# Moving parts of a weight conversion from ScalarE and VectorE to GpSimd and ScalarE, and chunk 1's attention behind chunk 0's, in a windowed attention with a feed-forward layer

## The chip, the cores and the metric

The kernel runs on one core of a Trainium2 chip. The metric is the device time of one execution in microseconds (us). The core's engines run side by side, each in its own order: PE multiplies matrices, DVE (VectorE), ACT (ScalarE) and POOL (GpSimd) work on tiles, and SP (SyncE) has nothing to do but to begin transfers. An engine starts an instruction only when the one before it in its order has started and everything that it needs is there.

## The reference

`q`, `k`, `v` have 8 batches, 8 heads, 576 positions and 64 features; `w_in` is 512 x 2048 and `w_out` 2048 x 512.

```python
scores = (q @ k.T) / sqrt(D) + slope[h] * -(i - j)      # kept where 0 <= i - j < 128
attn = softmax(scores) @ v
x = attn.transpose(0, 2, 1, 3).reshape(4608, 512)
h = x @ w_in
g = where(h >= 1, h, where(h <= -1, 0, (h + 1) ** 2 / 4))
out = g @ w_out
```

All tensors come in as 64-bit floats and the result is float32. The kernel reads a 64-bit number as two 32-bit words, a low one and a high one. `q`, `k` and `v` are used in float32 as they are loaded; only the weights are unfolded from the two words.

## The kernel before, in words

The 4608 tokens are worked in 12 chunks of 384 (`CH`). A chunk has 4 pairs of heads. For a pair: scores by PE (`scores`, L443; chunks from 2 on L459), the exponential with its maximum and sum by DVE and ACT (`soften`, L482 to L495), the transpose of the attention weights by PE (`weights_t`, L504), their copy by ACT (L508) and two masks by POOL (L509, L511), and the product with `v` by PE (`values`, L538). The four results of a chunk are its `x`, which is split into a high and a low half-precision part (L583, L584).

The feed-forward layer goes through 16 blocks of 128 hidden features. `layer1` makes 12 products (L590 to L592), the activation is done by ACT (L597) and DVE (L598, L599), and `layer2` adds 3 products (L619 in chunk 0, L622 to L624 later) into three accumulators.

The weights are converted while chunk 0 runs, block by block, and stay in memory. For a block `fc`: `fetch_weights` loads 512 KB of `w_in` and 512 KB of `w_out` into one of three buffers (`raw`, L173, L175, begun by ACT); `unfold` turns the high words (L180) and the low words (L181) on ACT; `float32_of` joins them on DVE (L185, once for `w_in` and once for `w_out`); DVE takes each row's largest magnitude of `w_in` (L194). `scale_in` finds the block's power of two: PE spreads the 128 row values over all partitions (`across`, L152), DVE takes the maximum and makes a scale of it (L159 to L163, L202). `split_in` then makes the two half-precision parts that `layer1` multiplies with (ACT L210, DVE L211). ACT adds up the magnitudes of `w_out`'s rows (L219).

The order on each engine is set by a list scheduler from the order in which the program is emitted and from "issue after" marks (`behind`). `segments` is the list of attention steps, `ready[c]` says how many of them chunk c's feed-forward layer needs, and the loop at the end spreads the next chunk's segments over the current chunk's 32 half steps. `EARLY` names the attention heads of chunk 0 behind which the first three blocks are converted; a later block `fc` is converted behind the activation of block `fc - 3` (`convert_after`). At the start PE runs idle transposes (`keep_busy`, L88).

## Time and profile before

| | us |
|---|---|
| median of 3 runs | 993.35 (991.59 to 994.22) |
| the profiled execution's own time | 991.8 |
| its span, first to last instruction | 989.7 |
| PE busy | 955.0 (96%) |
| DVE busy | 731.6 (74%) |
| ACT busy | 607.2 (61%) |
| POOL busy | 340.6 (34%) |

A busy PE says only that a matmul was under way. Three stages are told apart below: A, up to 44 us, is chunk 0's attention; B, from 44 to 152 us, is chunk 0's feed-forward layer with the conversion of the weights and chunk 1's attention; C is the rest, eleven chunks in which all weights are ready.

### The profile page before, as it was taken

The page shows a single profiled execution, that of the slowest core. Times are in us where ns is not written, and L with a number is a line of the kernel's source. Part 1 is how long each engine was busy: PE and PEld are TensorE (multiplying, and loading weights), DVE is VectorE, ACT ScalarE, POOL GpSimd, SP SyncE. Part 2 cuts the span into 40 slices and gives each one's busy share as a digit, 9 for nine tenths or more (in the row PEclk, how much of TensorE's full clock was granted, in tenths as well). Part 3 has the DMA queues.
Part 4 walks back from the last instruction along what each step waited for, and adds up shares of the span by engine and source line. Part 5 has one row for each costly group of instructions (what it writes and reads, how often), then busy time and mean ns, then how long its engine had stood idle before and what let it go on. Part 6 is the DMA issues. An engine that isn't in the chain of part 4 may idle for free.

```text
span 989.7 us, 17764 instructions
## 1 busy us (share of the span) xinstructions
PE 955.0 (96%) x6181; PEld 522.2 (53%) x6181; DVE 731.6 (74%) x2089; ACT 607.2 (61%) x1509; POOL 340.6 (34%) x446
## 2 busy tenths in 40 slices
PE   8798899998999999999999999999999999999997
PEld 5444344554555555555555555555555555555553
DVE  6899798896787787687787788677677886765332
ACT  6788777666656666565665665666666655644322
POOL 5311003333334432532533533433443443334221
PEclk9799999998999999999999999999999999999999
DMA  8476441012021011112111101111201000000000
GB/s 274 134 245 201 154 141 39 12 49 72 30 59 58 25 41 63 38 30 60 62 33 52 58 25 54 63 30 50 72 30 30 33 1 1 33 2 1 33 1 32
DMA packets 53290, 59.86 MB, mean 60 GB/s; under 512 B 3408, under 2 KB 42576, under 8 KB 53200
## 3 DMA queue, kind: packets, MB, share of 16 engines
q1 hardware_dynamic: 42304, 41.82, 13.7%
q10 hardware_dynamic: 10896, 16.91, 4.9%
q8 instruction: 48, 0.79, 0.3%
q14 instruction: 42, 0.34, 0.1%
HBM read 49.28 MB, written 9.44 MB: 59 GB/s over the span
## 4 chain that ended last, share of the span: by engine, by line
PE 85%; DVE 7%; ACT 4%; DMA 1%; issue 1%; POOL 1%; ACTq 0%; SPq 0%; POOLq 0%; DVEq 0%
PE h L590 12%; PE h L592 12%; PE h L591 12%; PE acc L622 12%; PE acc L623 12%; PE acc L624 12%; PE s L459 5%; PE x L561 4%; PE p L504 3%; ACT z L484 1%; PE acc L619 1%; DMA vn<-in_v_dram 1%; DVE g L598 1%; ACT raw L181 1%; DVE g L599 1%
## 5 line engine op out<-in xcount | busy, mean ns | idle before, releaser
L607 POOL TENSOR_TENSOR gl<-g,gh 128x384 f16<-128x384 f32 x176 | 167.2, 950 | 453.5 <-ACT gh L606 442.7
L598 DVE SCALAR_TENSOR_TENSOR g<-u,half 128x384 f32<-128x384 f32 x176 | 123.9, 705 | 157.1 <-ACT u L597 144.1
L606 ACT CAST gh<-g 128x384 f16<-128x384 f32 x176 | 89.6, 509 | 189.2 <-DVE g L599 102.1
L622 PE MATMUL acc<-wo,gh 128*128 128x512 f16 x528 | 200.3, 379 | 0.0
L623 PE MATMUL acc<-wo,gh 128*128 128x512 f16 x528 | 200.2, 379 | 0.0
L624 PE MATMUL acc<-wo,gl 128*128 128x512 f16 x528 | 196.0, 379 | 0.0
L597 ACT ACTIVATE u<-h,shift,fall 128x384 f32<-128x384 f32 x176 | 116.4, 663 | 98.9 <-PE h L592 98.9
L484 ACT ACTIVATE z<-z,nmax 128x256 f32<-128x256 f32 (+2 forms) x288 | 137.7, 480 | 33.1 <-DVE nmax L482 31.1
L590 PE MATMUL h<-x,wi 128*128 128x384 f16 x384 | 125.8, 329 | 4.6 <-ACT x L570 2.8
L590 PE MATMUL h<-xh,wi 128*128 128x384 f16 x384 | 125.2, 327 | 4.3 <-ACT wi L210 2.9
L592 PE MATMUL h<-xh,wi 128*128 128x384 f16 x384 | 125.3, 326 | 1.1 <-DVE wi L211 1.1
L592 PE MATMUL h<-x,wi 128*128 128x384 f16 x384 | 126.1, 328 | 0.0
L591 PE MATMUL h<-x,wi 128*128 128x384 f16 x384 | 126.0, 328 | 0.0
L591 PE MATMUL h<-xl,wi 128*128 128x384 f16 x384 | 125.4, 327 | 0.0
L482 DVE CUSTOM_DVE_ANT_0 z<-s,near,z_of 128x256 f32<-128x256 f32 (+2 forms) x240 | 98.6, 459 | 33.7 <-PE s L459 33.5
L599 DVE SCALAR_TENSOR_TENSOR g<-h,gain,g 128x384 f32<-128x384 f32 x176 | 108.1, 615 | 3.9
L590 PEld LDWEIGHTS <-wi 128*128 128x128 f16 x768 | 75.2, 98 | 67.1 <-issue 7.5
L591 PEld LDWEIGHTS <-wi 128*128 128x128 f16 x768 | 75.4, 98 | 59.1 <-issue 7.2
L592 PEld LDWEIGHTS <-wi 128*128 128x128 f16 x768 | 75.3, 98 | 53.9 <-issue 3.6
L519 POOL TENSOR_SCALAR_AFFINE_SELECT lu<-lu 128x768 f16<-128x768 f16 x80 | 70.4, 894 | 58.2 <-DVE lu L517 57.7
L624 PEld LDWEIGHTS <-gl 128*128 128x128 f16 x528 | 51.5, 98 | 59.0 <-issue 0.4
L622 PEld LDWEIGHTS <-gh 128*128 128x128 f16 x528 | 51.6, 98 | 51.0 <-issue 1.1
(148 smaller groups left out, 1445.7 us busy)
## 6 DMA issues: line engine op xcount, KB each, us to landing
out_dram<-o SPq DMA_DIRECT2D x35, 256.0 KB, 2.1
raw<-in_moe_w_in_dram ACTq DMA_DIRECT2D x16, 512.0 KB, 4.6
raw<-in_moe_w_out_dram ACTq DMA_DIRECT2D x16, 512.0 KB, 5.5
vn<-in_v_dram SPq DMA_DIRECT2D x32, 256.0 KB, 2.8
qk<-in_q_dram SPq DMA_DIRECT2D x40, 192.0 KB, 2.4
qk<-in_k_dram SPq DMA_DIRECT2D x28, 256.0 KB, 2.8
vn<-in_v_dram SPq DMA_DIRECT2D x16, 192.0 KB, 2.6
qk<-in_k_dram SPq DMA_DIRECT2D x12, 192.0 KB, 2.5
```

What stands on the lines that cost most here:

```text
L482: a = V.tensor_tensor_reduce(out=z[:, i, c0:], in0=pt[:, n, c0:], in1=r[:, c0:], op0=ALU.add, op1=ALU.min, scale=factor, scalar=3.0e38, ac ...
L484: b = S.activation(z[:, i, c0:], z[:, i, c0:], AF.Exp, bias=nmax[:, i:i + 1], scale=-1.0, accum_out=sm[:, i, 0:1])
L590: T.matmul(ph, wi[fc][:, 0, cc, :], xh, start=(cc == 0), stop=False)
L591: T.matmul(ph, wi[fc][:, 0, cc, :], xl, start=False, stop=False)
L592: T.matmul(ph, wi[fc][:, 1, cc, :], xh, start=False, stop=(cc == NCC - 1))
L597: first = S.activation(u, ph, AF.Relu, bias=shift[c] if c else quarter, scale=fall[c][:, col])
L598: V.scalar_tensor_tensor(g, u, half[c] if c else 0.5, u, ALU.min, ALU.mult)
L599: last = V.scalar_tensor_tensor(g, ph, gain[c][:, col] if c else fall[c][:, col], g, ALU.mult, ALU.max)
L607: G.tensor_tensor(gl, g, gh, ALU.subtract)
L622: T.matmul(a, gh[:, ts], wo[fc][:, 0], start=first, stop=False)
L623: T.matmul(a, gh[:, ts], wo[fc][:, 1], start=False, stop=False)
L624: T.matmul(a, gl[:, ts], wo[fc][:, 0], start=False, stop=last)
```

## The change

Five things change.

1. The low words of a block are scaled by POOL (`G.tensor_scalar`, 128 x 1024, unsigned integers in, integers out) and no longer by ACT.
2. All loads of weights are begun by SP, in one queue with the loads of `q`, `k` and `v`; block 0's are issued behind the loads of the first two pairs, with no wait for one of them to land. For blocks 1 and 2 a memset of two words by POOL holds the load to its place.
3. The rows of `w_in` are bounded by the sum of magnitudes, added up by ACT as for `w_out`, and no longer by their maximum on DVE. This gives another power of two, and so other roundings.
4. From block 2 on the power of two is found for two blocks at once, behind every second activation.
5. `values` of pairs 2 and 3 and the steps that chunk 0 still needs are emitted ahead of chunk 1's first scores; the maxima of chunk 1's `v` for pairs 4 to 7 are emitted together, after pair 4. `EARLY` is (2, 3, 4, 5, 6, 7) in place of (2, 3, 4, 5, 7, 8).

```diff
@@ -170,40 +170,52 @@
 
     def fetch_weights(fc):
         w = raw[fc] = rawp.tile([P, 2, DM, 2], I32, name=f"raw{fc}", tag=f"raw{fc % 3}")
-        S.dma_start(w[:, 0].rearrange("p (c f) w -> p c f w", c=NCC),
-                    wi32[:, 2 * fc * P:2 * (fc + 1) * P].rearrange("(c p) (f w) -> p c f w", p=P, w=2))
-        S.dma_start(w[:, 1], wo32[fc * P:(fc + 1) * P, :].rearrange("p (f w) -> p f w", w=2))
+        if 0 < fc < 3:
+            G.memset(w[:1, :, 0, :1], 0)
+        DMA.dma_start(w[:, 0].rearrange("p (c f) w -> p c f w", c=NCC),
+                      wi32[:, 2 * fc * P:2 * (fc + 1) * P].rearrange("(c p) (f w) -> p c f w", p=P, w=2))
+        DMA.dma_start(w[:, 1], wo32[fc * P:(fc + 1) * P, :].rearrange("p (f w) -> p f w", w=2))
 
     def unfold(fc, which=slice(0, 2)):
 
         low, high = raw[fc][:, which, :, 0], raw[fc][:, which, :, 1]
         S.activation(high.bitcast(F32), high.bitcast(F32), AF.Prelu, scale=2.0 ** -112, alpha=2.0 ** 32)
-        S.activation(low, low.bitcast(U32), AF.Copy, scale=0.9375 * 2.0 ** -29)
+        G.tensor_scalar(low, low.bitcast(U32), 0.9375 * 2.0 ** -29, None, ALU.mult)
 
     def float32_of(fc, a, out):
 
         V.scalar_tensor_tensor(out.bitcast(I32), raw[fc][:, a, :, 1], 3, raw[fc][:, a, :, 0], ALU.logical_shift_left, ALU.bitwise_or)
 
-    wide = {}
+    wide, rows_i = {}, {}
 
     def convert_in(fc):
         f = wide[fc] = wp.tile([P, DM], F32, name=f"f_i{fc}", tag="f_i", bufs=3)
         unfold(fc)
         float32_of(fc, 0, f)
-        rows = column(f"rows_i{fc}", "rows")
-        V.tensor_reduce(rows, f, X, ALU.max, apply_absolute_value=True)
-        spread(f"i{fc}", rows)
+        if fc < 2 or fc % 2 == 0:
+            width = 1 if fc < 2 else 2
+            rows_i[fc] = column(f"rows_i{fc}_{width}", f"rows{width}", n=width)
+        S.activation(junk, f, AF.Abs, accum_out=rows_i[fc] if fc < 2 else rows_i[fc - fc % 2][:, fc % 2:fc % 2 + 1])
 
     def scale_in(fc):
-        s1, i1 = s_in[:, fc:fc + 1], i_in[:, fc:fc + 1]
-        scale_of(f"i{fc}", s1, i1)
-
-    def fall_in(fc):
-        V.tensor_scalar(fall[0][:, fc:fc + 1], i_in[:, fc:fc + 1], i_x[0], 0.25, ALU.mult, ALU.mult)
+        rows = rows_i.pop(fc)
+        n = rows.shape[1]
+        s1, i1 = s_in[:, fc:fc + n], i_in[:, fc:fc + n]
+        b = bank(f"m_i{fc}")[:, :n * P]
+        across(b, rows)
+        top = column(f"top_i{fc}", f"top{n}", n=n)
+        V.tensor_reduce(top, b.rearrange("p (a w) -> p a w", w=P), X, ALU.max)
+        ti = top.bitcast(I32)
+        V.tensor_scalar(ti, ti, 0x7F800000, None, ALU.bitwise_and)
+        V.tensor_scalar(i1, top, 2.0 ** -100, 1.0 / TOP, ALU.max, ALU.mult)
+        V.reciprocal(s1, i1)
+        if fc > 1:
+            fall_in(fc, n)
+
+    def fall_in(fc, n=1):
+        V.tensor_scalar(fall[0][:, fc:fc + n], i_in[:, fc:fc + n], i_x[0], 0.25, ALU.mult, ALU.mult)
 
     def split_in(fc):
-        if fc > 1:
-            fall_in(fc)
         f, s1 = wide.pop(fc), s_in[:, fc:fc + 1]
         t = wp.tile([P, 2, DM], F16, name=f"wi{fc}", tag=f"wi{fc}")
         wi[fc] = t.rearrange("p s (c f) -> p s c f", c=NCC)
@@ -653,6 +665,12 @@
         turned[m] = len(segments)
 
     for p in range(p8):
+        if p == NPAIR:
+            segments.append([lambda p=p: values(p - 2)])
+            turn(2 * p - 2)
+            turn(2 * p - 1)
+            segments.append([lambda p=p: values(p - 1)])
+            ready.append(len(segments))
         segments += [[lambda p=p: scores(p, (0, 1))], [lambda p=p: scores(p, (2,))]]
         if p < NPAIR:
             segments.append([lambda p=p: behind([scored_at[p]], lambda: keep_busy(KEEP[2 if p else 1]))])
@@ -660,22 +678,21 @@
             segments.append([lambda p=p: in_turn(p + 1)] + ([lambda p=p: load_qk(p + 2)] if p + 2 < p8 else []))
         if p == NPAIR + 1:
             segments.append([lambda: scale_x(1)])
-        if 2 <= p <= NPAIR:
+        if 2 <= p < NPAIR:
             segments.append([lambda p=p: values(p - 2)])
-        if 1 <= p <= NPAIR:
+        if 1 <= p < NPAIR:
             turn(2 * p - 2)
             turn(2 * p - 1)
         if p >= NPAIR:
-            segments.append([lambda p=p: values(p - 1)])
-            if p == NPAIR:
-                ready.append(len(segments))
+            if p > NPAIR:
+                segments.append([lambda p=p: values(p - 1)])
             turn(2 * p)
             turn(2 * p + 1)
         d = 2 * p - (1 if p < NPAIR else 0)
         if p:
             segments += [[lambda d=d, x=x: behind(done_t[d], lambda: load_v(x, True))] for x in {1: (4, 5), 2: (6,), 3: (7,)}.get(p, ())]
             segments += [[lambda d=d, x=x: behind(done_t[d], lambda: load_all(x, True))] for x in {5: (8, 9), 6: (10,), 7: (11,)}.get(p, ())]
-            segments += [[lambda d=d, x=x: behind(done_t[d], lambda: reach_of(x))] for x in {3: (4, 5), 4: (6, 7), 6: (8,), 7: (9,)}.get(p, ())]
+            segments += [[lambda d=d, x=x: behind(done_t[d], lambda: reach_of(x))] for x in {4: (4, 5, 6, 7), 6: (8,), 7: (9,)}.get(p, ())]
     segments += [[lambda: behind(done_t[M1 - 2], lambda: reach_of(p8 + 2))],
                  [lambda: behind(done_t[M1 - 1], lambda: reach_of(p8 + 3))], [lambda: level(LIGHT)], [lambda: values(p8 - 1)]]
     ready.append(len(segments))
@@ -754,11 +771,11 @@
                 behind(done_g[f], lambda: fetch_weights(fc + 2))
             behind(done_g[f], lambda: convert_in(fc))
             behind(done_g[f - 1 if f else f], lambda: convert_out(fc))
-        if f + 2 < NFC:
+        if f + 2 < NFC and f % 2 == 0:
             behind(done_g[f], lambda: scale_in(f + 2))
 
 
-    EARLY = (2, 3, 4, 5, 7, 8)
+    EARLY = (2, 3, 4, 5, 6, 7)
     LEAD = len(EARLY) // 2
     KEEP = (14, 22, 6)
     STEPS = 2 * NFC
@@ -777,6 +794,7 @@
 
     load_first(0)
     load_first(1)
+    fetch_weights(0)
     load_v(0)
     load_first(2)
     load_v(1)
@@ -784,8 +802,6 @@
     load_v(2)
     load_v(3)
 
-    landed = S.copy(loaded, pair[0]["qr"][:, :1])
-    behind([landed.ins], lambda: fetch_weights(0))
     emit_attention(turned[0])
     behind(done_t[0], lambda: fetch_weights(1))
     for m in range(2, H + 1):
```

What this makes of the order is shown at three places. `lu_5`, `lu_6`, `lu_7` are the masked attention weights of heads 5 to 7 of chunk 0, `raw2` to `raw5` the weight buffers of blocks 2 to 5, `vn_7` a tile of `v`, `z_9` and `z_10` exponentials of chunk 1. The first place is POOL at the last masks of chunk 0, before:

```order
L509 AFFINE_SELECT lu_5_497<-lu_5_497 128x3x128
L511 AFFINE_SELECT lu_5_497<-lu_5_497 128x3x128
L376 MEMSET vn_7_517 1x1
L488 MEMSET z_9_537 128x64
L509 AFFINE_SELECT lu_6_582<-lu_6_582 128x3x128
L511 AFFINE_SELECT lu_6_582<-lu_6_582 128x3x128
L509 AFFINE_SELECT lu_7_597<-lu_7_597 128x3x128
L511 AFFINE_SELECT lu_7_597<-lu_7_597 128x3x128
L488 MEMSET z_10_706 128x64
```

and POOL at the same place in the change, whose lines are numbered 12 higher:

```order
L521 AFFINE_SELECT lu_5_498<-lu_5_498 128x3x128
L523 AFFINE_SELECT lu_5_498<-lu_5_498 128x3x128
L388 MEMSET vn_7_518 1x1
L183 TENSOR_SCALAR raw3_475<-raw3_475 128x1024
L521 AFFINE_SELECT lu_6_534<-lu_6_534 128x3x128
L521 AFFINE_SELECT lu_7_558<-lu_7_558 128x3x128
L523 AFFINE_SELECT lu_6_534<-lu_6_534 128x3x128
L183 TENSOR_SCALAR raw2_381<-raw2_381 128x1024
L523 AFFINE_SELECT lu_7_558<-lu_7_558 128x3x128
L183 TENSOR_SCALAR raw4_538<-raw4_538 128x1024
L183 TENSOR_SCALAR raw5_613<-raw5_613 128x1024
```

The low words of block 3 now stand ahead of heads 6 and 7, and those of block 2 ahead of the last mask.

The second place is PE in the same stretch; `s_8` and `s_9` are the scores of chunk 1's first pair, `x_2` and `x_3` the products with `v` of chunk 0's last two pairs, `p_6` and `p_7` the transposes of heads 6 and 7. Before:

```order
L443 MATMUL s_9_0_524<-kr_4_362,ql_4_451 128x256
L443 MATMUL s_8_0_523<-kr_4_362,ql_4_451 128x256
L443 MATMUL s_9_2_544<-kr_4_362,ql_4_451 128x192
L538 MATMUL x_2_569<-lu_5_497,vn_2_179 64x256
L538 MATMUL x_2_569<-lu_4_470,vn_2_179 64x256
L538 MATMUL x_2_569<-lu_5_497,vn_2_179 64x256
L538 MATMUL x_2_569<-lu_4_470,vn_2_179 64x128
L538 MATMUL x_2_569<-lu_5_497,vn_2_179 64x128
L443 MATMUL s_8_2_543<-kr_4_362,ql_4_451 128x192
L504 MATMUL p_6_578<-ident_85,ep_6_413 128x128 x3
```

PE there in the change:

```order
L550 MATMUL x_2_521<-lu_4_471,vn_2_182 64x256
L516 MATMUL p_6_530<-ident_85,ep_6_414 128x128 x3
L550 MATMUL x_2_521<-lu_5_498,vn_2_182 64x256
L550 MATMUL x_2_521<-lu_4_471,vn_2_182 64x256
L550 MATMUL x_2_521<-lu_5_498,vn_2_182 64x256
L550 MATMUL x_2_521<-lu_4_471,vn_2_182 64x128
L550 MATMUL x_2_521<-lu_5_498,vn_2_182 64x128
L152 LDWEIGHTS rows_i1_1_482
L152 MATMUL m_i1_547<-ident16_141,rows_i1_1_482 128x128
L516 MATMUL p_7_554<-ident_85,ep_7_421 128x128 x3
```

Chunk 1's scores are gone from here; they stand behind the first products of `layer1`, and the transpose of head 6 has moved ahead of most of `x_2`.

The third place is ACT in stage B, between the activations of two blocks (`u`); `rows_i` are the row bounds of `w_in`, `rows_o` those of `w_out`. Before:

```order
L180 ACTIVATE raw5_669<-raw5_669 128x1024
L181 ACTIVATE raw5_669<-raw5_669 128x1024
L508 COPY lu_11_861<-p_11_857 128x3x128
L597 ACTIVATE u_0_3_895<-h_0_3_882,quarter_91,fall0_509 128x384
L180 ACTIVATE raw6_777<-raw6_777 128x1024
L181 ACTIVATE raw6_777<-raw6_777 128x1024
L210 ACTIVATE wi4_872<-f_i4_780,s_in_143 128x512
L219 ACTIVATE junk_149,rows_o_148<-wf5_847 128x512
```

and ACT in the change:

```order
L609 ACTIVATE u_0_3_853<-h_0_3_840,quarter_91,fall0_510 128x384
L182 ACTIVATE raw6_722<-raw6_722 128x1024
L496 ACTIVATE z_10_741,sums_126<-z_10_741,nmax_10_742 128x192
L198 ACTIVATE junk_149,rows_i4_2_729<-f_i5_798 128x512
L231 ACTIVATE junk_149,rows_o_148<-wf5_803 128x512
L198 ACTIVATE junk_149,rows_i6_2_865<-f_i6_861 128x512
L595 ACTIVATE x_1_0_879<-x_4_870,s_x1_830 128x384
L231 ACTIVATE junk_149,rows_o_148<-wf6_867 128x512
L222 ACTIVATE wi4_827<-f_i4_725,s_in_143 128x512
```

Each block's pair of conversions is one conversion on ACT now, and a sum over `w_in` (L198) stands in ACT's order.

## Rows read from the trace of the kernel before

**Rows 1.** The page's part on the chain of work that ended last: shares of the span by engine.

```profile
PE 85%; DVE 7%; ACT 4%; DMA 1%; issue 1%; POOL 1%; ACTq 0%; SPq 0%; POOLq 0%; DVEq 0%
```

**Rows 2.** Busy time of each engine in the three stages: stretch, its length, busy us (and instructions) of PE, PE's weight load, DVE, ACT and POOL, the granted clock of TensorE (1.00 is 2.4 GHz), DMA share, GB/s.

```profile
0.00:44.00 44.00, 34.52 (x191) 22.25 (x192) 35.89 (x143) 30.84 (x90) 18.93 (x57) 0.88 0.72 229
44.00:152.00 108.00, 95.91 (x462) 48.44 (x461) 92.42 (x292) 84.84 (x176) 10.05 (x29) 0.98 0.52 172
152.00:990.00 838.00, 824.54 (x5532) 451.53 (x5529) 603.27 (x1656) 491.54 (x1246) 311.60 (x360) 1.00 0.12 37
```

**Rows 3.** The same view of two shorter stretches in which the granted clock was lower.

```profile
30.00:37.00 7.00, 7.00 (x27) 4.09 (x28) 6.82 (x30) 5.23 (x18) 1.38 (x4) 0.52 0.30 106
110.00:116.00 6.00, 5.52 (x16) 2.75 (x17) 4.66 (x12) 2.16 (x5) 0.00 (x0) 0.72 0.00 0
```

**Rows 4.** Who PE's matmuls waited for in stage B: us in total, times, longest.

```profile
PE acc L619 <- DVE g L599: 4.3, 4, 3.1
PE h L590 <- ACT wi L210: 2.9, 4, 1.6
```

**Rows 5.** The chain of work in stage B: its shares by line (the line is cut where the view cuts it), and, from a narrower stretch of it, two pieces (start us, us, what).

```profile
by line: PE acc L619 8.9%; ACT raw L181 7.0%; DVE wf L185 4.3%; DVE g L599 4.2%; ACT raw L180 4.2%; DVE g L598 4.2%; ACT u L597 4.2%; issue 3.9%; ACT z L484 3.8%; DVE z L482 3.7%; PE h L590 3.5%; DVE f_i L185 3.4%; PE h L591 3.1%; DMA vn<-i
...
101.60 1.06 ACT raw L180
102.67 1.04 ACT raw L181
```

**Rows 6.** The end of stage A: four pieces of the chain, then PE's and POOL's own instructions in order of time (start us, us, engine, line, operation; in brackets the idle time before, and what ended it).

```profile
17.07 6.17 DMA vn<-in_v_dram
...
23.34 0.69 DVE rows L385
...
29.93 2.94 PE s L443 x9
...
35.19 0.94 PE s L443 x2
...
36.05 0.87 PE L504 MATMUL p<-ident,ep 128*128 128x128 f32 x3
...
38.65 0.78 POOL L509 TENSOR_SCALAR_AFFINE_SELECT lu<-lu 128x384 f32<-128x384 f32 x1 [6.07 <-ACT lu L508]
...
41.65 2.23 PE L538 MATMUL x<-lu,vn 128*64 128x256 f32 x10 [0.26 <-POOL lu L511]
```

**Rows 7.** Groups of DVE's and ACT's instructions in stage B that the change touches: count, busy us, mean ns of one, idle time before.

```profile
L194 DVE TENSOR_REDUCE rows_i<-f_i 128x1 f32<-128x512 f32 x14 | 9.5, 678 | 0.0
L159 DVE TENSOR_REDUCE top_i<-m_i 128x1 f32<-128x128 f32 x14 | 3.9, 282 | 0.0
L482 DVE CUSTOM_DVE_ANT_0 z<-s,rel_end 128x256 f32<-128x256 f32 x6 | 2.5, 420 | 0.0
L202 DVE TENSOR_SCALAR fall<-i_in,i_x 128x1 f32<-128x1 f32 x14 | 2.7, 194 | 0.0
L385 DVE TENSOR_REDUCE rows<-vn 128x1 f32<-128x512 f32 x4 | 2.6, 676 | 0.4 <-DMA vn<-in_v_dram 0.4
L163 DVE RECIPROCAL s_in<-i_in 128x1 f32<-128x1 f32 x14 | 2.2, 157 | 0.3
L162 DVE TENSOR_SCALAR i_in<-top_i 128x1 f32<-128x1 f32 x14 | 2.1, 150 | 0.2
L161 DVE TENSOR_SCALAR top_i<-top_i 128x1 int32<-128x1 int32 x14 | 2.1, 148 | 0.1
...
L180 ACT ACTIVATE raw<-raw 128x1024 f32<-128x1024 f32 x13 | 14.9, 1147 | 1.1 <-issue 1.1
L181 ACT ACTIVATE raw<-raw 128x1024 int32<-128x1024 uint32 x13 | 14.7, 1132 | 0.0
L219 ACT ACTIVATE junk<-wf 128x512 bf16<-128x512 f32 x14 | 8.7, 623 | 2.9 <-DVE s_in L163 1.6 <-DVE top_i L161 1.3
L219 ACT ACTIVATION_READ_ACCUMULATOR junk<-wf 128x1 f32 x14 | 2.7, 191 | 0.0
```

**Rows 8.** POOL's nearest operations: the same operation on a smaller tile (shortest, median and longest ns, first and last start us), and the masks of chunks 0 and 1 (busy us, mean ns).

```profile
L127 POOL TENSOR_SCALAR rel<-rel x6: 847/847/1092, 4.4 to 9.0; 128x256 f32<-128x256 f32 x6
...
L509 POOL TENSOR_SCALAR_AFFINE_SELECT lu<-lu 128x384 f32<-128x384 f32 x16 | 9.6, 601 | 56.8 <-ACT lu L508 56.7
```

**Rows 9.** Two places, in order of time, where POOL worked beside a DVE instruction with two operands in on-chip memory: six scalings end at 9.83 us, and a mask at 31.66 us.

```profile
4.43 5.40 POOL L127 TENSOR_SCALAR rel<-rel 128x256 f32<-128x256 f32 x6
...
9.15 0.51 DVE L494 TENSOR_TENSOR z<-z 128x256 f32<-128x256 f32 x1 [0.90 <-ACT z L484]
...
9.72 0.41 DVE L494 TENSOR_TENSOR z<-z 128x256 f32<-128x256 f32 x1
...
31.14 0.52 POOL L509 TENSOR_SCALAR_AFFINE_SELECT lu<-lu 128x384 f32<-128x384 f32 x1 [3.59 <-ACT lu L508]
...
31.31 0.76 DVE L495 TENSOR_TENSOR ep<-z,rc 128x384 f32<-128x384 f32 x1
...
33.71 0.55 DVE L495 TENSOR_TENSOR ep<-z,rc 128x384 f32<-128x384 f32 x1
```

**Rows 10.** Transfers of the weights: all 16 of `w_in` (KB each, median us from issue to landing), and the issue of block 3's by ACT's queue.

```profile
raw<-in_moe_w_in_dram ACTq DMA_DIRECT2D x16, 512.0 KB, 4.6
...
26.43 0.39 ACTq L173 DMA_DIRECT2D raw<-in_moe_w_in_dram  x1
```

## The prediction

> **What bounds the kernel now.** I read the chain of work first: PE holds 85% of it, DVE 7%, ACT 4% [rows 1]. A change on POOL, ACT and DVE can therefore only win where PE waits, so the second view is the busy time by stage [rows 2]. In C PE is busy for 824.5 of 838.0 us at full clock, and the order of C is not touched by any of the five parts; I carry C over unchanged. In A PE is busy for 34.5 of 44.0, in B for 95.9 of 108.0. All that can be won is thus 9.5 us in A and 12.1 in B. In B DVE (92.4 busy, 15.6 idle) and ACT (84.8 busy, 23.2 idle) are close behind PE. Two shorter stretches show the granted clock at 0.52 from 30 to 37 us and 0.72 from 110 to 116 [rows 3], that is, wholly or partly at 1.2 GHz, where a product costs up to twice as much.
>
> Who holds PE in B: its accumulating products wait 4.3 us for the end of the activation on DVE, and the first products of a block 2.9 us for `split_in` on ACT [rows 4]. The chain through B names what lies behind these waits [rows 5]: low words L181 with 7.0% of 108 us = 7.6 us, high words L180 with 4.2%, and DVE's `wf`, `g` and `f_i` with 3 to 4% each. Both conversions stand end to end there, 1.06 and 1.04 us. So about 7.6/1.04 = 7 of B's 13 blocks have the low words on the chain. In A the chain goes through the last `v` transfer, its row maxima, two pieces of chunk 1's scores, the last four masks and the product with `v` [rows 6].
>
> **Low words on POOL, the largest term.** ACT loses 13 instructions of 1.132 us in B, 14.7 us [rows 7]. On the chain 7.6 us go. What comes in their place is POOL's operation on 128 x 1024, which the trace does not show. The same operation on 128 x 256 took 847 ns [rows 8]. Upper bound: four times that, 3.39 us. Lower bound: only the part in which POOL holds its input grows. The last of the six small scalings ends at 9.83, and DVE's operation with two inputs, begun at 9.15, took 0.51 where the next took 0.41 [rows 9]; it lost 0.10, so it ended its own wait near 9.24 while the scaling had begun at 9.83 - 0.85 = 8.98. That is 0.26 us of reading for 256 elements, 1.0 ns each, and 0.85 + 768 x 0.001 = 1.62 us. I take 1.62: the masks, which take 601 ns for 384 elements on the same engine [rows 8], also have a rate nearer 1 than 3.3 ns. POOL does it beside ACT's high words (pitch 1.06), so it sticks out by 1.62 - 1.06 = 0.56 in each of 7 blocks, 3.9 us. The chain in B gains 7.6 - 3.9 = 3.7 us. At 1.06 + 1.08 = 2.14 us for the operation the gain is nil; at 3.39 it is 7 x 2.33 = 16.3 - 7.6 = 8.7 us of loss.
>
> **What POOL takes from DVE.** DVE's joins L185, its scaling by a reciprocal and others have two inputs in on-chip memory. Next to a mask of 0.52 us such an operation took 0.76 in place of 0.55 [rows 9]; next to the scaling it lost 0.10. A hold is thus part of POOL's instruction, 0.26 for 256 elements or at most 1.04 for 1024. DVE meets it only if it has such an operation then; I take 0.7 for each of 13 blocks, 9.1 us (bounds: 0, when DVE does something else, and 13.5).
>
> The skill has a stronger rule. The Trainium skill (SBUF — State Buffer, section "SBUF: two separate sides") calls the port pair of DVE and GpSimd an exclusive lock, kept for the whole instruction by whoever starts first. The mask's row agrees with it; the scaling's does not, as DVE's operation ended at 9.66 inside the scaling's 8.98 to 9.83. By that rule the hold is the whole 1.62 us, 21 us in B where DVE has 15.6 idle; it is priced as a rival below.
>
> **DVE's and ACT's ledgers in B.** DVE loses the maxima of `w_in`, 9.5 us [rows 7]. One scale costs 282 + 148 + 150 + 157 + 194 = 0.93 us, and half of 14 go, 6.5 us less some 0.7 for a wider maximum: 5.8. It receives the holds, 9.1; chunk 1's first pair of scores, which moves over from A, with six operations of 420 ns, 2.5; and four maxima of `v` at 676 ns, 2.7 [rows 7]. Sum: -9.5 - 5.8 + 9.1 + 2.5 + 2.7 = -1.0. ACT loses 14.7 and receives 14 sums over `w_in` at 0.62 + 0.19 = 0.81, 11.4, and the moved exponentials, about 3.7 by estimate (six passes, each at most the 0.62 of the wider L219 [rows 7]): +0.4. So both stay as full as they were, and I credit no gain beyond the chain's. The sum of magnitudes stands behind `f_i` on ACT now, with what is queued there (activations of the next block) ahead of it; a scale for two blocks has a whole block more to come through, so this is covered. Without the cover the first products would wait 0.81 - 0.68 = 0.13 us longer in 14 blocks, 1.8 us.
>
> PE in B also receives the moved scores. In A they took 2.94 + 0.94 = 3.9 us on the chain at half clock [rows 3, 6], so about 2.0 at full clock; 12.1 us of idle take most of it, and I count 0.5. **B: -3.7 + 0.5 = -3.2.**
>
> **Stage A.** The scores leave the stretch ahead of the last transposes: 3.9 us. The row maxima of `v` for chunk 1, which wait for a transfer that lands at 17.07 + 6.17 = 23.24 and then take 0.69 of DVE's chain, move behind: another 1.5 by estimate, the 0.69 and the wait that DVE had for it. Gone: 5.4. Given back: POOL has block 2's low words ahead of the last mask, 1.62, and those wait on a chain that leads straight into the product with `v` [rows 6]. Block 3's stand ahead of the masks of heads 6 and 7, in the 6.07 us in which POOL waited [rows 6], but they need a transfer that could be begun only when POOL, not ACT, frees block 0's buffer; with 4.6 us from issue to landing after an issue that stood at 26.43 [rows 10], they end near 26.4 + 4.6 + 1.6 = 33 us plus the delay of the release. A delay of 3 us is free, and I count 0.7 for more. The holds of blocks 0 and 1 on DVE, which is on A's chain: 2 x 0.7 = 1.4. **A: -5.4 + 1.6 + 1.4 + 0.7 = -1.7.** Bounds: -5.4 if all is hidden, +3 if block 3's transfer lands after 36 us and the masks stand behind it.
>
> **Loads from SP.** The issue of 0.39 us leaves ACT [rows 10], but it stood beside ACT's work: ACT's conversions waited 1.1 us for "issue" in all of B [rows 7]. I count nothing. SP has no other work, so a transfer that waits on SP for its buffer holds only what stands behind it in the queue; three buffers lie between. If this cover goes, a block comes one landing late, 4.6 us, once.
>
> **Sum.** -3.2 - 1.7 = -4.9 on the profiled execution, 991.8, of which 2.1 lies around its span: 986.9. The median of the runs is 993.35, 1.55 above that execution; I forecast 993.35 - 4.9 = 988.4.
>
> **The rivals.** *More is won:* low words are never late, since blocks are converted three ahead, and PE's idle in B falls from 12.1 to about 6 while A keeps its 5.4. For: L181 is the longest non-PE entry of B's chain. Against: DVE's `g` [rows 4] is not relieved. 993.35 - 6 - 5.4 = 982. Chance 0.18.
>
> *Nothing is won:* low words leave the chain, and DVE takes their place with holds of 9.1 us and four more maxima; `g` waits 4.3 us already [rows 4]. PE idles as before, scores add 2.0 in B, and A gives 1.7 to 2.4: about 993. Chance 0.17.
>
> *Slower, the price of POOL's operation:* if it grows with its size from 847 ns, it is 3.39 us, and the chain in B loses 8.7 as above; A receives 1.8 more ahead of the last mask, and about nothing is left of its gain: 993.35 + 8.7 + 1.8 = 1004. It decides from 2.14 us on. For: the only row with this operation. Against: the reading takes 0.26 of its 0.85 us. Chance 0.13.
>
> *Slower, the lock for a whole instruction:* 13 holds of 3.39 - 0.7 = 2.69 more, 35 us on a DVE with 15.6 idle, 19 too many, and 4 in A from blocks 0 and 1 and the masks: 993.35 + 19 + 4 = 1016. With 1.62 in place of 3.39 it is 13 x 0.92 = 12 us more, inside DVE's idle time, and ends as the case in which nothing is won. Chance 0.05.
>
> **How the numbers follow.** The forecast has 0.47, with its own range of 984 to 993. What a measurement can tell from no change is 0.3%, 3.0 us: faster below 990.4, slower above 996.3. Faster: 0.18 and three quarters of 0.47, 0.54 with rounding. Same: 0.17 and most of the rest of the forecast's, 0.27. Slower: 0.13 + 0.05 + 0.01 = 0.19. The range of 979 to 1001 takes in the bigger gain and half of the case of 3.39 us, and leaves the lock out.
>
> **What would show it.** The mean of POOL's 128 x 1024 operation: 1.6 as taken, above 2.1 the sum's sign turns. DVE's joins: a longest one 0.7 above the shortest bears out the holds, a join that ends together with POOL's operation the lock. The chain in B without low words, or with POOL's in their place; PE's idle there near 9. Chunk 0's first product of `layer1` near 42 us and not at 41.65 + 2.23 = 43.9 [rows 6]. ACT's busy time in B within 1 us of 84.8. Half-clock stretches in A that end earlier, as PE has less idle time ahead of them. The prediction is wrong if C's length differs by more than 1 us, if POOL's last masks in A wait for block 3's transfer, or if DVE's busy time in B rises by more than its 15.6 idle.

## The result and the profile after

The changed kernel takes 998.4 us in the median of 5 runs (996.96 to 999.13), 1.0053 times the time before (95% interval 1.0039 to 1.0068), which had a median of 993.1 in the 5 runs beside it: slower by 5.3 us. The forecast was 988.4, faster by 4.9. The profiled execution took 998.46, its span is 996.7.

The windows view, cut where chunk 0's and chunk 1's first products of `layer1` start (columns as in [rows 2]):

```profile
0.00:48.20 48.20, 31.69 (x178) 19.99 (x179) 32.26 (x117) 27.38 (x80) 32.34 (x62) 0.80 0.63 202
48.20:152.70 104.50, 91.05 (x431) 45.37 (x431) 84.86 (x241) 77.16 (x181) 43.97 (x43) 0.98 0.52 174
152.70:996.70 844.00, 831.18 (x5574) 455.27 (x5573) 610.59 (x1682) 497.36 (x1264) 311.41 (x360) 0.99 0.12 38
35.00:40.00 5.00, 1.48 (x7) 0.68 (x5) 4.22 (x10) 3.39 (x9) 2.69 (x1) 0.50 0.88 297
40.00:45.00 5.00, 1.12 (x2) 0.29 (x2) 0.30 (x1) 0.00 (x0) 4.78 (x6) 0.50 0.03 12
```

The kernel before, cut at the same two products:

```profile
0.00:43.80 43.80, 34.32 (x189) 22.12 (x189) 35.69 (x143) 30.76 (x89) 18.93 (x57) 0.88 0.72 230
43.80:145.60 101.80, 89.72 (x433) 45.32 (x433) 86.22 (x263) 80.56 (x160) 10.05 (x29) 0.98 0.54 179
145.60:989.70 844.10, 830.93 (x5563) 454.76 (x5561) 609.67 (x1685) 495.91 (x1261) 311.60 (x360) 1.00 0.12 37
```

So A grew by 4.4 us, B by 2.7 (101.8 to 104.5), and C stayed (844.1 to 844.0). In A PE's idle time rose from 9.5 to 48.2 - 31.7 = 16.5 us, and the last two rows of the first list show where: from 35 to 45 us PE is busy for 2.6 us of 10, at half clock, and from 40 to 45 only POOL works. In B DVE fell from 86.2 to 84.9 us of work and ACT from 80.6 to 77.2: both engines behind PE became lighter, and the stage became longer. (The fixed stretch of [rows 2], 44 to 152 us, shows larger falls, to 85.8 and 77.9, but in the changed kernel its first 4 us still belong to A.)

POOL in that stretch of A, in order of time (the counterpart of the masks in [rows 6]):

```profile
28.19 3.22 POOL L183 TENSOR_SCALAR raw<-raw 128x1024 int32<-128x1024 uint32 x1
...
37.31 2.87 POOL L183 TENSOR_SCALAR raw<-raw 128x1024 int32<-128x1024 uint32 x1 [4.18 <-DVE i_in L210]
40.25 0.99 POOL L521 TENSOR_SCALAR_AFFINE_SELECT lu<-lu 128x384 f32<-128x384 f32 x2
41.20 0.52 POOL L523 TENSOR_SCALAR_AFFINE_SELECT lu<-lu 128x384 f32<-128x384 f32 x1
41.80 2.87 POOL L183 TENSOR_SCALAR raw<-raw 128x1024 int32<-128x1024 uint32 x1
44.74 1.03 POOL L523 TENSOR_SCALAR_AFFINE_SELECT lu<-lu 128x384 f32<-128x384 f32 x1
```

Block 3's low words stand at POOL's head until 37.31, then block 2's go ahead of the last mask. The last mask starts at 44.74 where it started at 41.08 before:

```profile
41.08 0.52 POOL L511 TENSOR_SCALAR_AFFINE_SELECT lu<-lu 128x384 f32<-128x384 f32 x1
```

SP's issue of block 3's load, and PE's wait for the last mask, from the same trace:

```profile
30.22 0.38 SPq L175 DMA_DIRECT2D raw<-in_moe_w_in_dram  x1
...
31.20 0.50 SPq L177 DMA_DIRECT2D raw<-in_moe_w_out_dram  x1
...
45.83 2.39 PE L550 MATMUL x<-lu,vn 128*64 128x256 f32 x10 [2.94 <-POOL lu L523]
```

The load is begun at 30.22 where it was begun at 26.43 [rows 10]. It needs block 0's buffer, which comes free when DVE has joined block 0's `w_out`: at 28.57 + 1.57 = 30.14 now, at 25.71 + 0.68 = 26.39 before. Block 0's low words end at 25.82 on POOL where they ended at 22.75 on ACT, and the join itself, shown below, is 0.89 longer. The releaser that the view names for 37.31, a small DVE instruction, does not feed these low words. The issue of 31.20 has its own landing in the trace, 5.6 us later, and that fits: 31.20 + 5.6 = 36.8. Block 2's load had begun at 22.53 and landed by 27.60; its low words only stood behind block 3's.

POOL's new operation, over the first 152 us, beside [rows 8]:

```profile
L183 POOL TENSOR_SCALAR raw<-raw 128x1024 int32<-128x1024 uint32 x16 | 48.5, 3029 | 32.6 <-DMA raw<-in_moe_w_out_dram 28.0 <-DVE i_in L210 4.2
```

It takes 3.03 us, near the upper bound of 3.39. But 28.0 of the 32.6 us that POOL waits before it are waits for a landing: in B POOL mostly has the operation's input late. DVE's joins are seen to wait for the operation once, 5.2 us before the start at 44.70, in A.

What it takes from DVE shows at a join beside POOL's low words of 28.19 to 31.41, and at an instruction on two elements a row (L210) beside those of 121.12 to 124.12:

```profile
28.57 1.57 DVE L187 SCALAR_TENSOR_TENSOR wf<-raw 128x512 int32<-128x512 int32 x1
30.07 0.55 DVE L507 TENSOR_TENSOR ep<-z,rc 128x384 f32<-128x384 f32 x1
```

```profile
L210 DVE TENSOR_SCALAR i_in<-top_i x9: 154/170/1085, 31.5 to 145.4; 128x2 f32<-128x2 f32 x7, 128x1 f32<-128x1 f32 x2
...
121.24 1.08 DVE L210 TENSOR_SCALAR i_in<-top_i 128x2 f32<-128x2 f32 x1
```

The join needs 0.68 alone and took 1.57, a loss of 0.89; the operation after it has two inputs too and runs at its full speed while POOL is still at work. So in these two places POOL holds DVE near its start and not for its length. One slow instruction of DVE does not fit: L209, also on two elements, took 0.76 us for its usual 0.16 when it began 2.2 us after POOL, at 64.12.

### The profile page after: what moved, and what is told of

Read it like the earlier page. It is cut to its first block, busy times and chain, and to the rows that moved or that the text cites. A ratio compares the mean times of both kernels' runs of the same rounds, so it can differ in the third digit from the quotient of the medians.

```text
span 996.7 us, 17795 instructions
## 1 busy us (share of the span) xinstructions
PE 953.9 (96%) x6181; PEld 520.6 (52%) x6181; DVE 727.7 (73%) x2038; ACT 601.9 (60%) x1524; POOL 387.7 (39%) x464
## 4 chain that ended last, share of the span: by engine, by line
PE 82%; DVE 2%; ACT 1%; issue 0%; DVEq 0%; ACTq 0%
PE h L602 12%; PE h L604 12%; PE acc L634 12%; PE h L603 12%; PE acc L635 12%; PE acc L636 11%; PE s L471 5%; PE x L573 4%; PE p L516 2%; PE acc L631 1%; DVE g L610 0%; ACT o L647 0%; ACT z L496 0%; DVE g L611 0%; ACT u L609 0%
## 5 line engine op out<-in xcount | busy, mean ns | idle before, releaser
L609 ACT ACTIVATE u<-h,shift,fall 128x384 f32<-128x384 f32 x176 | 116.4, 664 | 98.1 <-PE h L604 97.7
```

Of the source, the lines that this page charges most:

```text
L609: first = S.activation(u, ph, AF.Relu, bias=shift[c] if c else quarter, scale=fall[c][:, col])
```

## The experiments

Times are ratios to the kernel before, with the 95% interval; the three last columns are read from one profiled execution each: the start of chunk 0's first product of `layer1` (the end of A), the length of B up to chunk 1's, and the time of that execution, which can lie several us beside the median behind the ratio. For part 5 alone it is 992.0 where the median is 995.2, for parts 1, 2, 3 it is 1000.0 where the median is 993.9. So A and B say where an execution spent its time, and the ratio what a part costs.

| kernel | ratio | interval | A, us | B, us | execution, us |
|---|---|---|---|---|---|
| before | 1 | | 43.8 | 101.8 | 991.8 |
| + low words (1) | 1.0017 | 1.0006 to 1.0028 | 45.1 | 97.4 | 992.8 |
| + loads (2) | 0.9991 | 0.9979 to 1.0004 | 44.0 | 98.3 | 992.1 |
| + sums (3) | 0.9967 | 0.9955 to 0.9980 | 43.3 | 98.9 | 990.3 |
| + scales for two (4) | 1.0042 | 1.0028 to 1.0055 | 44.0 | 107.8 | 996.9 |
| + moved attention (5) | 1.0026 | 1.0013 to 1.0038 | 37.6 | 104.5 | 992.0 |
| the changed kernel | 1.0053 | 1.0039 to 1.0068 | 48.2 | 104.6 | 998.5 |
| without 1 | 1.0040 | 1.0025 to 1.0055 | 42.6 | 110.2 | 998.2 |
| without 1 for blocks 0 to 3 | 1.0040 | 1.0026 to 1.0054 | 43.5 | 107.1 | 995.1 |
| low words of 2, 3 behind the masks | 1.0046 | 1.0028 to 1.0064 | 38.3 | 110.2 | 994.9 |
| without 4 | 1.0047 | 1.0031 to 1.0064 | 47.6 | 101.2 | 994.3 |
| without 4, and 1 for 0 to 3 | 0.9999 | 0.9979 to 1.0020 | 42.3 | 100.4 | 991.5 |
| without 5 | 1.0016 | 1.0001 to 1.0031 | 50.6 | 103.2 | 996.7 |
| before + a part of 4's wait | 1.0001 | 0.9988 to 1.0014 | 42.6 | 103.3 | 989.5 |
| before + 2, 3 | 0.9958 | 0.9944 to 0.9973 | 43.8 | 97.6 | 988.4 |
| before + 2, 3, and 1 from block 4 on | 0.9943 | 0.9925 to 0.9962 | 43.5 | 100.5 | 985.5 |
| before + 1, 2, 3 | 1.0013 | 0.9994 to 1.0032 | 52.4 | 99.0 | 1000.0 |
| before + 3, 4 | 1.0110 | 1.0089 to 1.0131 | 43.3 | 114.7 | 1003.8 |
| before + 5, maxima of v in their old place | 0.9981 | 0.9968 to 0.9994 | 43.0 | 97.7 | 990.7 |
| without 4, and 1 for 0 to 3, maxima in their old place | 1.0013 | 1.0000 to 1.0025 | 44.6 | 99.1 | 992.4 |

In C the twenty executions differ too, but only at its start: from chunk 3's first product of `layer1` to the end each of them takes 683.1 to 683.9 us. Between chunk 1's first product and chunk 3's lies a wait of its own. PE stands before the scaled `x` of chunk 2, here before the change and with part 5 alone:

```profile
235.25 0.80 PE L590 MATMUL h<-x,wi 128*128 128x384 f16 x2 [2.83 <-ACT x L570]
236.75 0.80 PE L590 MATMUL h<-x,wi 128*128 128x384 f16 x2 [1.08 <-ACT x L570]
```

With part 5 alone chunk 1's first product is 3.4 us earlier, chunk 2's `x` 1.5 us later, and chunk 3's first product stands at 306.5 where it was at 306.1. So a stage that is shorter in A and B need not make the kernel faster.

### Part 1, undone three ways, and alone

My first theory was POOL's queue in A; the rivals were the holds on DVE, and the other four parts. Part 1 undone:

```diff
-        G.tensor_scalar(low, low.bitcast(U32), 0.9375 * 2.0 ** -29, None, ALU.mult)
+        S.activation(low, low.bitcast(U32), AF.Copy, scale=0.9375 * 2.0 ** -29)
```

> The changed kernel with the low words of all 16 blocks back on ScalarE; the other four parts stay. In the changed kernel's trace chunk 0's first product of layer1 starts at 48.2 us where it was 43.8, with GpSimd's masks standing behind the low words of blocks 3 and 2. Theory (GpSimd's queue): stage A heals to 44 us or less, B keeps the moved scores, time about 993. Rival 1 (what counts is that GpSimd's operation holds VectorE, about 1 us in each of 16 blocks): A and B both heal, about 990 or less. Rival 2 (the slowdown comes from the other four parts, the low words are neutral): 997 or more.

The same under `if fc < 4`, POOL for the rest:

> The changed kernel with the low words of blocks 0 to 3 alone back on ScalarE, those of blocks 4 to 15 on GpSimd. Theory (GpSimd's queue ahead of chunk 0's masks): the whole loss of A comes back, first product of layer1 at 44 us or earlier, time 993 to 995. Rival 1 (holds on VectorE): 12 of 16 holds stay, 996 to 997. Rival 2 (other parts): 997 or more.

The order alone; its second line moves the whole conversion of block 2, and the load of block 4, from behind head 6 to behind head 7:

```diff
-        G.tensor_scalar(low, low.bitcast(U32), 0.9375 * 2.0 ** -29, None, ALU.mult)
+        behind(done_t[H - 1] if fc in (2, 3) else [], lambda: G.tensor_scalar(low, low.bitcast(U32), 0.9375 * 2.0 ** -29, None, ALU.mult))
-    EARLY = (2, 3, 4, 5, 6, 7)
+    EARLY = (2, 3, 4, 5, 7, 7)
```

> The changed kernel, all low words on GpSimd, but those of blocks 2 and 3 are marked to stand behind the last masks of chunk 0. Nothing is left out. Theory (queue): the masks no longer wait, the first product of layer1 starts 3 to 5 us earlier, at 43 to 45 us; blocks 2 and 3 come later, which B may give back in part: 994 to 996. Rival 1 (holds): the holds stay, 998. Rival 2 (other parts): 998.

And part 1 alone on the kernel before:

> The kernel before with the low words on GpSimd and nothing else changed. In its order the low words of block 3 stand ahead of the masks of heads 6 and 7. Theory (queue): A loses 2 to 4 us, B stays or gains up to 3 by the shorter conversion, about 995. Rival 1 (holds): VectorE had 15.6 us idle in B and takes 13 holds of about 1 us while its maxima stay, so B loses 5 or more: 1000 or more. Rival 2 (low words neutral): 993.

Measured 1.0040, 1.0040, 1.0046 and 1.0017. A healed as the theory said, to 42.6, 43.5 and even 38.3 us. The time hardly did: where A became 5.6, 4.7 and 9.9 us shorter, B became 5.6, 2.5 and 5.6 longer, 107 to 110 us. So A's end alone is not what sets B's, and the theory falls as the explanation of the sum, while the holds as a cause of 5 us or more fall with the last run. The first products of `layer1` in the run with the low words behind the masks:

```profile
L602 PE MATMUL h<-x,wi x72: 322/326/337, 148.5 to 238.4; 128*128 128x384 f16 x72
L602 PE MATMUL h<-xh,wi x64: 326/326/527, 38.2 to 146.5; 128*128 128x384 f16 x64
```

The second row is chunk 0, which starts 9.9 us earlier than in the changed kernel; the first row is where chunk 1 starts, at 148.5 where it is 152.7: 4.2 of the 9.9 are left.

### The other parts, each alone on the kernel before

Part 5 is its hunks as they stand; part 2 likewise; part 3 is one line, and part 4 keeps the maxima on DVE:

```diff
-        V.tensor_reduce(rows, f, X, ALU.max, apply_absolute_value=True)
+        S.activation(junk, f, AF.Abs, accum_out=rows)
```

> The kernel before with part 5 alone (chunk 1's attention behind chunk 0's, the maxima of v together, the new table of heads). With the low words back on ScalarE the changed kernel still took 1.0040 times the time before, with A 1.2 us shorter and B 8.5 us longer. Theory (the moved attention fills B): A ends 2 to 5 us earlier, B takes 6 to 9 us longer since the first pair of chunk 1 with its exponentials now lies there, time 996 to 997. Rival (scales for two blocks make the first products wait): this part costs nothing, 992 to 994.

> The kernel before with the power of two found for two blocks at once, and nothing else (the maxima stay on VectorE). Theory (the moved attention): VectorE saves 5.8 us, time 991 to 993. Rival (scales for two blocks): a block's scale waits until the next block is converted, PE waits longer for split_in (2.9 us before), B 4 to 8 us longer, time 996 or more.

> The kernel before with the rows of w_in bounded by ScalarE's sums, and nothing else (the power of two may differ, and so the roundings). VectorE loses 9.5 us in B, ScalarE, with 84.8 of 108.0 us busy, takes 11.4. Theory (the moved attention is the cause): 993 to 994. Rival (ScalarE was next to full and becomes the bound): B 3 to 6 us longer, time 996 to 998.

> The kernel before with all loads of weights begun by SP and nothing else; block 0's no longer wait for a landing. Theory (the moved attention is the cause): within 1 us of before, 992 to 994. Rival (loads of q, k and v stand behind waiting loads of weights in SP's one queue, or share the transfers' rate): A 1 to 4 us longer, time 995 or more.

Measured 1.0026, 1.0042, 0.9967 and 0.9991. Both theories hold in part: the moved attention costs, and the scales for two blocks cost more. The sums do not fill ACT: they are the one part that clearly gains, 3.3 us. The five ratios add to +4.3 us, close to the 5.3 measured, which suggested that the parts simply add. The next runs tried that.

### Do the parts add?

> The changed kernel with part 4 undone: a power of two for each block by itself, the sums on ScalarE stay. Alone on the kernel before, the parts moved the median by about +1.7 us (low words), -0.9 (loads), -3.3 (sums), +4.2 (scales for two blocks), +2.6 (moved attention). Theory (the scale for two blocks is the largest cost, since the first block of a pair waits for the second's conversion, and the parts add): 993.5 to 995. Rival (GpSimd's queue in A is the larger cost here, and B's end does not hang on the scales): 997 or more.

A part of the wait of part 4, without its savings:

```diff
+        maxed[fc] = V.tensor_reduce(rows, f, X, ALU.max, apply_absolute_value=True).ins
...
-            behind(done_g[f], lambda: scale_in(f + 2))
+            behind(done_g[f] + ([maxed[f + 3]] if f % 2 == 0 else []), lambda: scale_in(f + 2))
```

> The kernel before, a scale for each block by itself with all its instructions, but the scale of each even block from 2 on is marked to stand behind the row maximum of the next block, as a scale for both would. It has the wait of part 4 and none of its savings. Theory (the wait is the cost of part 4): VectorE's 5.8 us are not saved either, so at least as slow as with part 4 alone, 995.5 to 998. Rival (the cost is in the wider tiles, or in the two splits that then stand together): 992 to 994.

> The kernel before with parts 2 and 3 alone, the loads from SP and the sums on ScalarE. Theory (the parts add): 0.9967 and 0.9991 give about 0.996 of before, 988 to 989.5. Rival (both gain from the same stretch): 989.5 to 991.

> Parts 2 and 3 with the low words on GpSimd for blocks 4 to 15 only, so that no low words stand ahead of chunk 0's masks. Theory (low words cost by GpSimd's queue in A and relieve ScalarE in B): as fast as parts 2 and 3 alone or up to 3 us faster, 986 to 989. Rival (in B they cost too, by about 1 us for which VectorE is held in each block, or by 3.0 us in place of 1.1 on a block's way): 990 to 993.

Without part 4 the changed kernel stays at 1.0047: they don't add. The run with the wait gives 1.0001, but it holds back less than part 4 does. There only DVE's share of an even block's scale stands behind the next block's row maximum; PE has spread that block's rows over the partitions before. With part 4 the spreading too comes after it. Part 4 alone first, then the run with the wait, both around blocks 4 and 5:

```profile
69.76 0.68 DVE L196 TENSOR_REDUCE rows_i<-f_i 128x1 f32<-128x512 f32 x1
70.50 0.23 PE L152 MATMUL m_i<-ident,rows_i 128*128 128x128 bf16 x1
72.41 0.41 DVE L205 TENSOR_REDUCE top_i<-m_i 128x2 f32<-128x256 f32 x1
```

```profile
66.68 0.67 DVE L194 TENSOR_REDUCE rows_i<-f_i 128x1 f32<-128x512 f32 x1
67.27 0.28 DVE L159 TENSOR_REDUCE top_i<-m_i 128x1 f32<-128x128 f32 x1
```

In the first, DVE takes up the scale 2.0 us after the row maximum has ended, behind block 6's joins; in the second it does so at once. So this run does not show that part 4 costs by something other than its wait. Parts 2 and 3 give 0.9958, and with the low words of blocks 4 to 15 on POOL 0.9943, the fastest kernel of the study, 6.4 us ahead of the kernel before by the medians and 5.7 by the ratio. The intervals of these two kernels overlap (0.9944 to 0.9973, and 0.9925 to 0.9962): from block 4 on the move to POOL, with POOL's 3.03 us and ACT's relief together, costs nothing that can be told.

### Two causes that hide each other

> The changed kernel with two things undone at once: a power of two for each block by itself, and the low words of blocks 0 to 3 on ScalarE. Each alone left it at 1.0047 and 1.0040 of before. Theory (two bounds that hide each other: GpSimd's queue ahead of chunk 0's masks in A, and the scales for two blocks in B; whichever is undone, the other still holds): both undone, 988 to 991. Rival (the moved attention is what costs, whatever the others do): 994 or more.

> The changed kernel with part 5 undone (parts 1 to 4 on the kernel before). Alone part 5 cost 2.6 us. Theory (two bounds that hide each other, neither of them part 5): 996 to 998. Rival (the moved attention is what costs): 991 to 994.

> Parts 1, 2 and 3 on the kernel before, the low words of all blocks on GpSimd. With blocks 0 to 3 on ScalarE it took 0.9943 of before. Theory (the first four blocks' low words cost by GpSimd's queue ahead of the masks in A): 3 to 5 us slower than that, 990 to 992, with the first product of layer1 2 to 4 us later than 43.5. Rival (where they stand in A doesn't matter, since stage B takes it up): 986 to 988.

> Parts 3 and 4 on the kernel before, sums on ScalarE and a scale for two blocks. Alone they gave 0.9967 and 1.0042; the wait of part 4 without its scales gave 1.0001. Theory (part 4 costs by itself wherever it stands): the parts add, 993 to 995. Rival (part 4 cost only since VectorE's maxima stood between a block's join and its scale): 988 to 990.

Part 4 and the first four blocks' low words, each undone, give back 0.6 and 1.3 thousandths; both undone give 5.4 (1.0053 to 0.9999), though the time, 992.4, is a little above the 988 to 991 that I expected. That both together are the loss is shown. That they hide each other is the likely reading: the 3.5 thousandths by which the two together give more than their sum are just beyond what the four intervals allow. What part 4 does is visible in these traces as well: from block 4's first product to block 14's it takes 64.5 us before, 67.1 in the changed kernel, and, with the first four blocks' low words on ACT, 66.8 with part 4 and 62.3 without it. Whether the low words of blocks 0 to 3 cost by the queue ahead of the masks, by the later release of block 0's buffer or by the holds on DVE is not separated: no run changes their order with part 4 undone. Without part 5 the ratio is 1.0016, between the two expectations.

With parts 2 and 3 in place, the low words of blocks 0 to 3 cost 0.9943 to 1.0013, 7 us by themselves. The profiled execution of this kernel was the slowest of its runs, 1000.04, but shows the place:

```profile
38.78 2.94 POOL L183 TENSOR_SCALAR raw<-raw 128x1024 int32<-128x1024 uint32 x1 [1.98 <-DVE nmax L484]
...
43.49 2.91 POOL L183 TENSOR_SCALAR raw<-raw 128x1024 int32<-128x1024 uint32 x1 [1.56 <-DMA raw<-in_moe_w_out_dram]
46.47 1.00 POOL L511 TENSOR_SCALAR_AFFINE_SELECT lu<-lu 128x384 f32<-128x384 f32 x2
47.42 1.86 POOL L513 TENSOR_SCALAR_AFFINE_SELECT lu<-lu 128x384 f32<-128x384 f32 x2
```

There the low words that stand ahead of the last four masks wait for their landing until 43.49, and all four masks behind them.

Parts 3 and 4 together gave 1.0110: what costs 4.2 us alone costs 14 with the sums on ACT. ACT and DVE around the second pair's scale there, ACT first:

```profile
66.96 1.12 ACT L180 ACTIVATE raw<-raw 128x1024 f32<-128x1024 f32 x1
67.98 1.13 ACT L181 ACTIVATE raw<-raw 128x1024 int32<-128x1024 uint32 x1
...
69.55 1.17 ACT L180 ACTIVATE raw<-raw 128x1024 f32<-128x1024 f32 x1
...
70.58 1.14 ACT L181 ACTIVATE raw<-raw 128x1024 int32<-128x1024 uint32 x1
...
71.60 0.64 ACT L196 ACTIVATE junk<-f_i 128x512 bf16<-128x512 f32 x1
...
76.92 1.32 ACT L220 ACTIVATE wi<-f_i,s_in 128x512 f16<-128x512 f32 x2
```

```profile
69.14 0.69 DVE L185 SCALAR_TENSOR_TENSOR f_i<-raw 128x512 int32<-128x512 int32 x1 [0.83 <-ACT raw L181]
...
74.55 0.43 DVE L205 TENSOR_REDUCE top_i<-m_i 128x2 f32<-128x256 f32 x1 [1.50 <-PE m_i L152]
...
75.95 0.16 DVE L209 RECIPROCAL s_in<-i_in 128x2 f32<-128x2 f32 x1
```

Block 5's conversion starts at 66.96, its join ends at 69.83, its row sum has to wait on ACT until 71.60 behind block 6's two conversions, the scale of blocks 4 and 5 is there at 76.11, and both splits follow at 76.92. Block 4 was joined long before and can't go. The products of block 4 start at 77.68 us and those of block 14 at 148.73, five such rounds of 14.2 us; in the kernel with the sums alone they start at 70.91 and 134.10, 12.6 us for two blocks. The program says why: block f + 3 is converted behind the activation of block f; with a scale for two, the same conversion must be through before block f + 2 can be multiplied. The loop from activation to activation closes over two blocks and no longer three. This trace has the low words on ACT. With all of them on POOL part 4 costs nothing measurable (1.0013 without it, 1.0016 with it), but there the first four blocks' low words cost as well and may hide it: with those four on ACT it costs 4.1 thousandths (0.9999 without it, 1.0040 with it). That POOL's share makes part 4 cheap is thus not shown.

### What in part 5 costs

In the trace of part 5 alone DVE and PE, with block 3's conversion:

```profile
45.80 0.69 DVE L185 SCALAR_TENSOR_TENSOR f_i<-raw 128x512 int32<-128x512 int32 x1 [0.31 <-ACT raw L181]
...
47.62 2.46 DVE L385 TENSOR_REDUCE rows<-vn 128x1 f32<-128x512 f32 x4
49.99 0.68 DVE L194 TENSOR_REDUCE rows_i<-f_i 128x1 f32<-128x512 f32 x1
...
51.77 0.75 DVE L211 SCALAR_TENSOR_TENSOR wi<-f_i,s_in,wi 128x512 f16<-128x512 f32 x1
```

```profile
49.50 0.34 PE L590 MATMUL h<-xh,wi 128*128 128x384 f16 x1 [1.99 <-ACT wi L210]
...
52.58 0.50 PE L592 MATMUL h<-xh,wi 128*128 128x384 f16 x1 [2.58 <-DVE wi L211]
```

The four maxima of `v` stand in a row ahead of block 3's row maximum and DVE's share of block 2's split, and PE waits 2.6 us for that share. The 2.0 us before it are a wait for ACT's share, which starts at 48.71, behind block 4's conversion on ACT. Both last runs keep part 5 but put the maxima where they were:

```diff
-            segments += [[lambda d=d, x=x: behind(done_t[d], lambda: reach_of(x))] for x in {4: (4, 5, 6, 7), 6: (8,), 7: (9,)}.get(p, ())]
+            segments += [[lambda d=d, x=x: behind(done_t[d], lambda: reach_of(x))] for x in {3: (4, 5), 4: (6, 7), 6: (8,), 7: (9,)}.get(p, ())]
```

> Part 5 alone on the kernel before, but the maxima of chunk 1's v stay where they were (two after pair 3, two after pair 4). In the trace of part 5 alone the four maxima take VectorE 2.46 us in a row from 47.62 us, ahead of block 3's row maximum, and PE waits 2.0 and 2.6 us for block 2's split there. Theory (the four maxima together give back what A gained): part 5's cost of 2.6 us goes, 991 to 993. Rival (the moved scores cost, since chunk 1's first pair lies where B is full): 994 to 996.

> The changed kernel with single scales, low words of blocks 0 to 3 on ScalarE, and the maxima of chunk 1's v where they were. Without the last edit 0.9999 of before; without part 5 altogether 0.9943. Theory (four maxima together): 0.994 to 0.997, 987 to 990. Rival (the moved scores): 0.998 or more, 991 or more.

On the kernel before, 1.0026 became 0.9981: there the four maxima are the whole cost of part 5, and without them it gains. They also are what had shortened A: with them in their old place A ends at 43.0 us and no longer at 37.6. On the other kernel 0.9999 became 1.0013: nothing is gained, and the theory falls there. With parts 2 and 3, and 1 from block 4 on, in place, part 5 costs 5.6 thousandths (0.9943 to 0.9999). Which piece of it does so stays open, but the traces show the place, and it is not in A or B: chunk 1's first product is at 142.7 with part 5 and at 143.9 without it, chunk 3's at 306.7 and 300.4. PE's wait for chunk 2's scaled `x`, from 150 to 320 us, with part 5 and without it:

```profile
PE h L595 <- ACT x L575: 2.8, 2, 1.7
PE h L595 <- ACT x L575: 0.3, 1, 0.3
```

No run tests whether this wait makes the whole difference.

## Why the prediction was wrong

**C unchanged, and the place of all effects in A and B:** right for this pair, 844.1 against 844.0, while A, forecast to lose 1.7, grew by 4.4 and B, forecast to lose 3.2, by 2.7. For the parts it does not hold: in the profiled executions of the other kernels C takes 839.8 to 848.3 us, and how much of a shorter A and B is left shows only at chunk 3's first product.

**Low words, price.** "I take 1.62" was the first step to fail: 3.03. The bounds held it; the choice between them did not. I took the rate from how long POOL held DVE, 0.26 us in 0.85, and took the rest for a fixed part. From 128 x 256 to 128 x 1024 it grew by (3.029 - 0.847) / 768 = 2.8 ns an element: most of that rest grows too, and a hold is not a rate. The smaller operation has float32 numbers and the larger one unsigned integers, and no run separates the type from the size.

**Low words, place.** The rival with 3.39 us had the sign right, from the wrong place: it put the loss on seven blocks in B. From block 4 on the move costs nothing that can be told (0.9958 to 0.9943). The loss is in A, where I gave back 1.6 + 1.4 + 0.7 = 3.7; with parts 2 and 3 in place, blocks 0 to 3 cost 7 by the ratios. The term that failed most is "a delay of 3 us is free, and I count 0.7 for more": block 3's load began 3.8 us later, the low words, forecast to end near 33, started at 37.31, and four masks stood behind them, the last of these behind block 2's low words as well. My bound of +3 for A spoke of this case; A grew by 4.4.

**The hold on DVE.** Taken 0.7, bounded by 1.04; measured 0.89 on the join. The rule of the Trainium skill that was weighed (SBUF — State Buffer, section "SBUF: two separate sides") would have kept the join waiting until 31.41, POOL's end; it ended at 28.57 + 1.57 = 30.14. The trace does not agree with a lock for the whole instruction here. The mask's row, which I read as agreeing, does so only roughly: a wait until 31.66 and 0.55 behind it would have ended at 32.21, and the operation ended at 32.07. What was missed is that an instruction on two elements with one input is caught as well (1.08 in place of 0.17, its median), and that a hold delays the release of a buffer: the 0.89 us on block 0's join are part of the 3.8 us by which block 3's load was late.

**The ledgers of DVE and ACT.** DVE's -1.0 was near (86.2 to 84.9 in B), ACT came out lighter than the +0.4 forecast (80.6 to 77.2), and neither said anything about the time. That they hold no gain "beyond the chain's" was wrong both ways: the sums alone gain 3.3 us, and the scales for two, which save instructions, lose 4.2.

**Scales for two blocks.** "A scale for two blocks has a whole block more to come through, so this is covered" is the step that failed here. It is the other way round: the first block of a pair loses the block of lead that it had. With the sums and the low words on ACT, whose queue holds the next block's conversions ahead of the sum, the cost was 14 us where I had 1.8 for the lost cover. In the changed kernel, where the low words are on POOL, it gives back 0.6 thousandths when undone alone and 4.1 when the first four blocks' low words are undone as well. Why it costs 4.2 us with the maxima on DVE is not settled, since the run that was to test it holds back only a part of the wait.

**Stage A's gain.** The moved attention alone ended A at 37.6, 6.2 us earlier, against 5.4 forecast. That the two are near is luck. I had 3.9 for the scores and 1.5 for the maxima; with the maxima in their old place A ends at 43.0, only 0.8 earlier, and with part 5 alone eight products of chunk 1's scores still stand ahead of the last product with `v`:

```profile
34.49 1.66 PE L443 MATMUL s<-kr,ql 64*128 64x256 f32 x8
```

That the gain shortens the whole was wrong. In that execution B takes up 2.8 of the 6.2 us, where the conversion of block 3 and the split of block 2, not A's end, release the products that follow, and C takes up the rest and more (844.1 to 848.1).

**The loads.** Counted as nothing; 0.9991 (0.9979 to 1.0004) does not contradict it.

## What to carry to other kernels

Before an operation is moved to an engine with time to spare, look at what stands behind it in that engine's queue when its input is late: here a late transfer held four masks, and the spare time counted for nothing. Where the work goes round in a loop (convert, scale, multiply, activate, convert again), count over how many blocks the loop closes; a batch that joins two blocks shortens the lead by one, and here that outweighed the instructions saved. When one part undone gives little back, undo two at once: two causes can hide each other. And before a shorter stage is counted as won, look for the place from which on all variants take the same time: here that is chunk 3's first product, and what lies before it swallowed a gain of over 3 us.

## What the runs showed of the hardware that was not expected

GpSimd's scaling of 128 x 1024 unsigned integers took 2.87 to 3.27 us, mean 3.03, against 847 ns for 128 x 256 numbers in float32. In the places shown it delays VectorE near its start: the join lost 0.89 us beside it, and the next operation with two inputs, from 30.07 on and still inside POOL's 28.19 to 31.41, took 0.55, its usual time. VectorE's instruction on 128 x 2 with a single input, 0.17 us in the median, took 1.08 when it began 0.12 us after GpSimd's; another of this size took 0.76 for 0.16 when it began 2.2 us after.
